# Places of matrices in SBUF: v in products of 448 columns, and the gate's sums by GpSimd and DVE

## The chip, the cores and the metric

The kernel runs on one core of a Trainium2 chip. The metric is the device time of one execution in microseconds (us), the median of several runs. Everything is computed in float32 accuracy. Most products are made from float32r operands that are split in two parts, a high one (the value rounded to float32r) and a low one (the rest), so that one float32 product becomes three float32r products: high by high, high by low, low by high.

## What is computed

```python
x = A_x                                            # 1 x 2048 x 448
g = sigmoid((x * gate_w).sum(-1, keepdims=True))   # one gate for each token
qkv = x @ wqkv                                     # 16 heads of 28
p = softmax(q @ k.T * 28 ** -0.5)
a = (p @ v) @ wo
y = layernorm(x)
b = gelu(y @ w1 + b1) @ w2 + b2                    # 448 -> 1792 -> 448
out = g * a + (1 - g) * b
```

## The kernel before

The tokens are worked in four chunks of 512 (`NC`, `CH`), or in 16 tiles of 128 (`NT`). The kernel has three stages, and within each the order of the instructions on every engine is written out by hand; semaphores alone tie the engines together.

**Stage 1, q, k and v** (to 114 us). For each chunk there are seven tiles of q and k (`qk_tile`, 11 products of 128x512 each, line 220; the first chunk's are at line 322, piece by piece as the data arrives) and four tiles of v (`v_tile`, 11 products each, line 232). In `v_tile` the tokens are the stationary matrix (128x128) and the weights the moving one, 450 columns wide: 448 of v, one with `gate_w`, so that the gate's sum falls out of the same product (line 235 copies it to `zall`), and one of padding. The high and low parts of v's weights lie in two tensors, `wvh` and `wvl`, each with four pieces (of the 448 rows, in 128s) at a distance of 512 columns, that is 2048 bytes in a partition. Beside the products, a list (`at(n, ...)`) puts other work into the slots between the tiles n = 7 to 43: loads and splits of the next chunk's x, the layer norm's statistics by DVE from the token tiles (`stats_fetch`, `ln_stats`, lines 253 and 254), and the first pieces of the MLP's weights. DMAs are issued by SyncE (SP) in program order.

**Stage 2, the MLP** (to 467 us). For each chunk: 14 tiles `mlp1` (11 products of 512 columns, line 613) and then four `mlp2`, one for each 128 tokens. `mlp2` runs over f = 0 to 13 with three products of 448 columns for each f: moving `w2h[f]` with stationary `hh[f]` (line 626), moving `w2l[f]` with stationary `hh[f]` (line 627), moving `w2h[f]` with stationary `hl[f]` (line 631). The places in SBUF follow from the order of allocation: `w2h0, w2l0, w2h1, w2l1, ...`, of 1792 bytes each up to f = 10 and 2048 bytes from f = 11, and `hh[f], hl[f]` of 2048 bytes each from f = 13 down to 0, with a pad of 256 bytes ahead of f = 10 and one of 64 bytes ahead of f = 6 (`SHIFTS`). So `w2h[f]` starts at 0 and `w2l[f]` at 256 within a grid of 512 bytes up to f = 10, and at 0 both from f = 11. `hh[f]` and `hl[f]` start 64 bytes off a grid of 256 bytes for f = 0 to 6, and on it for f = 7 to 13.

Between the MLP's products stand *fillers*: products of q and k whose maxima by row the softmax needs later (line 440; in the MLP stage in bursts of six, `MG`; DVE reduces them, lines 420 and 422). They begin in the first chunk at f = `FS`. Fillers read `khr`, whose load is issued by GpSimd at f = 1 of the first chunk (line 503).

**Stage 3, attention** (to 1097 us, and a tail to 1112 us). Units of (group of heads, query chunk, key tile, head) are worked in rounds of five (`U`), later of seven. A round has three kinds of score products, each 28 or 29 rows deep, several side by side on different row groups of TensorE (line 563): stationary `khi` with moving `qh`, stationary `klo` with moving `qh`, stationary `khi` with moving `ql`; first for the round's first units, then for the last ones. ScalarE takes the exponentials (line 567, two a round). Then follow the products with v (line 830). Fillers stand in this stage too. The projection by `wo` (lines 735 to 737, 12 products of 448 columns for each 128 tokens, moving `woh[g]`, `wol[g]`, `woh[g]`) comes in the last quarter.

All matrices of stage 3, those of `mlp1` and those of q and k start on a grid of 512 bytes. `woh[g]` and `wol[g]` start at the same place within 512 bytes, 0 for g = 0 and 2, 256 for g = 1 and 3.

Of the kernel before, what the change touches and what calls it, by code (L numbers as in the profile page):

```python
# [15 lines left out]
P = 128  # L16
S = 2048
D = 448
# [4 lines left out]
CH = 512  # L23
# [7 lines left out]
MLP_MAX = 482  # L31
MLP_G = MLP_MAX // 260
MG = 6
FS = 4
WARM = 10
W1, W2 = 0.233, 0.205
SHIFTS = {10: 64, 6: 16}
LQ = 12
STEPS = (2, 5, 7, 8, 9, 10)
LSTEPS = (1, 3, 5, 6, 7, 8)  # L40
# [3 lines left out]
def kernel(ctx: ExitStack, tc: tile.TileContext, xt, wqk, wv, wo, xk, w1, b1, w2, b2,  # L44
                          ident_d, sel_d, out):
    nc = tc.nc

    const = ctx.enter_context(tc.tile_pool(name="const", bufs=1))
    dram = ctx.enter_context(tc.tile_pool(name="dram", bufs=1, space=DRAM))
# [6 lines left out]
    zall = const.tile([P, NT], F32, name="zall")  # L56
# [6 lines left out]
    vs = dram.tile([NT, P, NG, P], F32, name="vs")  # L63
    lns = dram.tile([2 * NT, P], F32, name="lns")
    gbs = dram.tile([NT, P, D], F32, name="gbs")
    ones = dram.tile([S // P, P], F32, name="ones")
    rls = dram.tile([NG * NC, 4, CH], F32, name="rls")

# [14 lines left out]
    w1h, w1l, w2h, w2l = {}, {}, {}, {}  # L83
# [73 lines left out]
    with tc.tile_pool(name="qx", bufs=2) as qx, tc.tile_pool(name="qo", bufs=4) as qo, \  # L157
# [8 lines left out]
        def raw():  # L166
            return qx.tile([P, CH], F32, name="raw", bufs=6)
# [14 lines left out]
            nc.scalar.activation(wh[:, m], wt[m], AF.Copy)  # L182
            nc.gpsimd.tensor_sub(wl[:, m], wt[m], wh[:, m].bitcast(F32))

        wvh, wvl = (qw.tile([P, 4, CH], F32R, name=f"wv{x}")[:, :, :450] for x in "hl")
        vt = [qw.tile([P, H, 32], F32, name=f"vt{i}") for i in range(3)]

        xh, xl = {}, {}
        xraw = {}

        def fetch_x(c, t):
            xraw[c, t] = raw()
            nc.sync.dma_start(xraw[c, t], xt[t, :, c * CH:(c + 1) * CH])
# [29 lines left out]
        def v_tile(tt):  # L223
            c, i = divmod(tt, TPC)
            sl = slice(i * P, (i + 1) * P)
            ps = next_ps()
            ops = []
            for t in range(3):
                ops += [(xh[c][:, t, sl], wvh[:, t]), (xh[c][:, t, sl], wvl[:, t]), (xl[c][:, t, sl], wvh[:, t])]
            ops += [(xh[c][:, 3, sl], wvh[:, 3]), (xh[c][:, 3, sl], wvl[:, 3])]  # L230
            for k, (a, b) in enumerate(ops):
                nc.tensor.matmul(ps[:, :450], a, b, start=(k == 0), stop=(k == len(ops) - 1))  # L232
            v = vt[tt % 3]
            nc.scalar.activation(v[:, :, 0:DH], ps[:, :D].rearrange("p (h d) -> p h d", d=DH), AF.Copy)
            nc.vector.tensor_copy(zall[:, tt:tt + 1], ps[:, D:D + 1])
            nc.sync.dma_start(vs[tt], v.rearrange("p (g j) d -> p g (j d)", g=NG))

        one_t = qw.tile([S // P, P], F32, name="one_t")
# [2 lines left out]
        mv = qw.tile([P, NT, 2], F32, name="mv")  # L241
        mr = qw.tile([P, 2, NT], F32, name="mr")

        bxr = {}

        def stats_fetch(i):
            bxr[i] = spare(i % (NF // 2)).rearrange("p a b -> p (a b)")[:, :2 * D].rearrange("p (t d) -> p t d", d=D)
            nc.sync.dma_start(bxr[i], xk[2 * i:2 * i + 2].rearrange("t p d -> p t d"))

        def ln_stats(i):  # L250
            x = bxr.pop(i)
            for n in range(2):
                nc.vector.bn_stats(st[:, 2 * i + n], x[:, n])
                nc.vector.bn_aggr(mv[:, 2 * i + n], st[:, 2 * i + n])

# [34 lines left out]
        wvr = []  # L290
# [2 lines left out]
            nc.sync.dma_start(wvr[t], wv[:, t])  # L293
        for t in range(2):
            fetch_x(1, t)
        for v in vt:
            nc.gpsimd.memset(v[:, :, DH:DH + 1], 1.0)
            nc.gpsimd.memset(v[:, :, DH + 1:32], 0.0)
        banks = [next_ps() for m in range(NM)]
        there, pieces, late, count = [], [], [], [0] * NM  # L300
        for what, i in turns:
            if what == "w":
                if i < 4:
                    split_wqk(i)
# [12 lines left out]
            ops += [("hl", m, t) for m, t in new if t < 3]  # L317
            if i == NM - 1:
                ops += late
            for k, m, t in ops:  # L320
                w, x = wl if k == "lh" else wh, xl[0] if k == "hl" else xh[0]
                nc.tensor.matmul(banks[m], w[:, m, t], x[:, t], start=(count[m] == 0), stop=(count[m] == 10))  # L322
                count[m] += 1
                if m == 0 and count[m] == 11:

                    for n in range(4, NM):
                        split_wqk(n)
                    for n in range(4):
                        nc.scalar.activation(wvh[:, n], wvr[n], AF.Copy)
                        nc.gpsimd.tensor_sub(wvl[:, n], wvr[n], wvh[:, n].bitcast(F32))  # L330
                if count[m] == 11:
                    qk_out(0, m, banks[m])
                    if m in (1, 3):
                        split_x(1, m // 2)
                        fetch_x(1, m // 2 + 2)
# [5 lines left out]
        def at(n, what, *args, to=behind):  # L341
            to[n].append((what, args))
# [6 lines left out]
                at(11 * (c - 1) + 4 + t, split_x, c, t)  # L349
        for i, n in enumerate((11, 12, 13, 14, 19, 20, 21, 22)):  # L350
            at(8 + i if i < 7 else 13, stats_fetch, i, to=ahead)
            at(n, ln_stats, i)
        for t, d in ((ident, ident_d), (b1s, b1), (ones, one_t)):
            at(16, nc.sync.dma_start, t, d, to=ahead)
# [15 lines left out]
        for n in range(NM, 11 * NC):  # L370
            for what, a in ahead[n]:
                what(*a)
            c, m = divmod(n, 11)
# [157 lines left out]
    qs = {}  # L531

    def load_q(n):

        g, c = divmod(n, NC)
        qs[n] = aq.tile([P, CH], F32R, name="qh", bufs=3), aq.tile([P, CH], F32R, name="ql", bufs=3)
        for i in range(2):
            for j in range(4):
                r = (4 * g + j) * DH
                nc.sync.dma_start(qs[n][i][32 * j:32 * j + DH].bitcast(F32), qk[i, r:r + DH, c * CH:(c + 1) * CH])  # L540
# [52 lines left out]
    mw2 = ml.enter_context(tc.tile_pool(name="mw2", bufs=1, reuse_waits="tile"))  # L593
    mh = ml.enter_context(tc.tile_pool(name="mh", bufs=1, reuse_waits="tile"))
    for f in range(NF):
        w2h[f], w2l[f] = (mw2.tile([P, CH if f > 10 else D], F32R, name=f"w2{x}{f}")[:, :D] for x in "hl")
    hh, hl = {}, {}
    more = [mh.tile([P, CH], F32, name=f"more{i}") for i in range(2)]
    for f in reversed(range(NF)):
        if f in SHIFTS:  # L600
            mh.tile([P, SHIFTS[f]], F32, name=f"shift{f}")
        hh[f] = mh.tile([P, CH], F32R, name=f"hh{f}")
        hl[f] = mh.tile([P, CH], F32R, name=f"hl{f}")

# [35 lines left out]
    with texts:  # L640
# [12 lines left out]
        for c in range(NC):  # L653
            for f in range(NF):
                if c == 0:
# [21 lines left out]
            if c == NC - 1:  # L677
                m0.close()
                aq = ctx.enter_context(tc.tile_pool(name="aq", bufs=1, side="right", reuse_waits="tile"))
# [36 lines left out]
    aw = sb("aw", 1)  # L716
    ao = sb("ao", 2)
    woh = aw.tile([P, NG, D], F32R, name="woh")
    wol = aw.tile([P, NG, D], F32R, name="wol")

    b2b = aw.tile([P, D], F32, name="b2b")
    sel = aw.tile([P, P], F32, name="sel")

    outcome = [[aw.tile([P, S], F32R, name=f"o{x}{g}") for x in "hl"] for g in range(NG - 1)]
    acc = {}

# [18 lines left out]
    def finish(g, c, pv):  # L745

        ob = ao.tile([P, CH], F32, name="ob")
        rc = ao.tile([P, CH], F32, name="rc")
        lt = ao.tile([P, CH // 32], F32, name="lt")
        nc.vector.tensor_copy(ob, pv)  # L750
        nc.gpsimd.dma_start(lt, ob[DH:P:32, :])  # L751
        yield True
        nc.vector.reciprocal(lt, lt)
        r = rls[g * NC + c]
        nc.gpsimd.dma_start(r.rearrange("j (a b) -> (j a) b", b=CH // 32), lt)
        for j in range(4):
            nc.gpsimd.dma_start(rc[32 * j:32 * j + 32], r[j].partition_broadcast(32))
        yield True
        if g < NG - 1:
            oh, ol = (x[:, c * CH:(c + 1) * CH] for x in outcome[g])  # L760
        else:
            oh, ol = ao.tile([P, CH], F32R, name="oh", bufs=1), ao.tile([P, CH], F32R, name="ol", bufs=1)
# [72 lines left out]
    with tc.manual_schedule(engines=ENGINES):  # L835
# [3 lines left out]
        at = -1  # L839
# [3 lines left out]
        while u < 4 * steps:  # L843
# [56 lines left out]
            if ended:  # L900
                n = summed // NT - 1
# [62 lines left out]
```

## Time and profile before

| | us |
|---|---|
| runs before (3), median (lowest to highest) | 1114.77 (1114.1 to 1116.31) |
| the profiled execution | 1114.39 |
| span of its profile, first to last instruction | 1112.6 |
| TensorE busy in the span | 1104.5 |
| DVE busy | 741.3 |
| ScalarE busy | 634.7 |
| GpSimd busy | 334.2 |

In the profile PE is TensorE's products and PEld its loads of stationary matrices, which run beside the products. Products are pipelined: the duration that the profile gives for one product, 360 ns and more, holds its latency too. What a product costs in a dense row is the *step*, the distance from its start to the next one's start. In the views below the first two numbers of a row are the start and the length in us, "x" is a count, and a bracket says how long the engine had idled before and what ended that.

### The profile page before, as it was taken

The numbers are of one execution on the slowest core, as the hardware profiler recorded it, in microseconds if no ns is written. First come the engines' busy times: TensorE is split into PE (matmuls) and PEld (weight loads), VectorE is DVE, ScalarE is ACT, GpSimd is POOL, SyncE is SP. The second block draws the span as 40 slices with busy tenths as digits, with TensorE's granted clock in tenths as the row PEclk, the third lists the DMA queues.
The fourth block names the chain that finished last, engine by engine and source line by source line (L and its number), as shares of the span: only waits on it lengthen the run. The fifth ranks groups of instructions, "written<-read, shape, count | busy, mean of one in ns | idle before, by whom it ended". The sixth has DMA issues, their size and how long they took to land.

```text
span 1112.6 us, 19807 instructions
## 1 busy us (share of the span) xinstructions
PE 1104.5 (99%) x8156; PEld 675.4 (61%) x8156; DVE 741.3 (67%) x1030; ACT 634.7 (57%) x660; POOL 334.2 (30%) x354
## 2 busy tenths in 40 slices
PE   9999999999999999999999999999999999999998
PEld 7888777777777767744444444444444444454545
DVE  4553488988988889576676766667667667746103
ACT  5334640331240232287887887877878878847572
POOL 5025664343334331013112221320223024342350
PEclk9999999999999999999999999999999999999999
DMA  7988641011121022162100220012011003002111
GB/s 266 356 275 272 177 123 44 9 47 46 41 56 37 25 63 77 52 159 77 28 20 19 61 75 18 20 28 53 29 56 37 18 20 94 12 26 70 51 36 59
DMA packets 53079, 84.35 MB, mean 76 GB/s; under 512 B 8516, under 2 KB 28500, under 8 KB 52076
## 3 DMA queue, kind: packets, MB, share of 16 engines
q1 hardware_dynamic: 48732, 76.27, 22.0%
q0 software_dynamic: 4256, 6.81, 2.5%
q8 instruction: 64, 1.05, 0.4%
q14 instruction: 27, 0.22, 0.1%
HBM read 56.40 MB, written 26.49 MB: 75 GB/s over the span
## 4 chain that ended last, share of the span: by engine, by line
PE 98%; DVE 1%; ACT 1%; DMA 1%; issue 0%; SPq 0%; ACTq 0%
PE bank L830 22%; PE bank L563 20%; PE bank L440 16%; PE bank L613 13%; PE bank L220 5%; PE bank L631 5%; PE bank L626 4%; PE bank L627 4%; PE bank L232 3%; PE bank L322 1%; PE bank L735 1%; PE bank L736 1%; PE bank L737 1%; DMA raw<-in_xt 1%; ACT khi L567 0%
## 5 line engine op out<-in xcount | busy, mean ns | idle before, releaser
L567 ACT ACTIVATE pt<-bank 128x1536 f32<-128x1536 f32 (+1 forms) x386 | 460.1, 1242 | 121.8 <-PE bank L563 121.8
L420 DVE TENSOR_REDUCE mx<-bank 128x1 f32<-128x512 f32 x618 | 409.6, 687 | 174.3 <-PE bank L440 160.1
L830 PE MATMUL bank<-pt,vg 128*32 128x512 f32 x1942 | 260.4, 602 | 0.0
L422 DVE TENSOR_REDUCE mx<-bank 128x2 f32<-128x1024 f32 x203 | 238.8, 1219 | 29.9 <-PE bank L440 29.6
L440 PE MATMUL bank<-khi,qd 28*128 28x512 f32 x512 | 241.8, 480 | 0.1
L440 PEld LDWEIGHTS bank<-khi,qd 28*128 28x128 f32 x512 | 92.6, 182 | 148.1 <-DVE mx L420 106.0
L563 PE MATMUL bank<-qh,klo 28*128 28x512 f32 x1024 | 174.3, 394 | 0.0
L563 PE MATMUL bank<-qh,khi 29*128 29x512 f32 x768 | 156.5, 481 | 0.8 <-ACT khi L567 0.6
L613 PE MATMUL bank<-y,w1f 128*128 128x512 f32 x616 | 151.9, 398 | 0.0
L613 PEld LDWEIGHTS bank<-y,w1f 128*128 128x128 f32 x616 | 112.7, 188 | 33.1 <-issue 10.9
L563 PE MATMUL bank<-ql,khi 28*128 28x512 f32 x768 | 129.1, 390 | 0.0
L618 POOL TENSOR_TENSOR hl<-h,hh 128x512 fp32r<-128x512 f32 x56 | 72.9, 1301 | 117.6 <-ACT h L617 77.5
L616 ACT ACTIVATE hh<-bank,b1s 128x512 fp32r<-128x512 f32 x56 | 38.6, 689 | 99.0 <-PE bank L613 97.5
L830 PEld LDWEIGHTS bank<-pt,vg 128*32 128x32 f32 x1942 | 44.7, 108 | 78.5 <-issue 78.0
L563 PEld LDWEIGHTS bank<-qh,klo 28*128 28x128 f32 x1024 | 87.5, 185 | 3.5
L637 ACT ACTIVATE h<-bank 128x448 f32<-128x448 f32 x16 | 8.7, 546 | 137.5 <-PE bank L631 103.3
L751 POOL DMA_DIRECT2D lt<-ob x15 | 10.9, 725 | 252.6 <-DVE ob L750 252.6
L631 PE MATMUL bank<-w2h,hl 128*128 128x448 f32 x224 | 84.9, 379 | 0.0
L563 PEld LDWEIGHTS bank<-qh,khi 29*128 29x128 f32 x768 | 60.7, 182 | 39.6 <-ACT pt L567 24.9
L626 PE MATMUL bank<-w2h,hh 128*128 128x448 f32 x224 | 83.2, 371 | 0.0
L627 PE MATMUL bank<-w2l,hh 128*128 128x448 f32 x224 | 81.8, 365 | 0.0
L440 PE MATMUL bank<-khr,qd 28*128 28x512 f32 x512 | 80.4, 467 | 0.9 <-issue 0.7
(135 smaller groups left out, 1296.5 us busy)
## 6 DMA issues: line engine op xcount, KB each, us to landing
qk<-hl SPq DMA_DIRECT2D x28, 512.0 KB
raw<-in_xt SPq DMA_DIRECT2D x16, 256.0 KB
vs<-vt SPq DMA_DIRECT2D x16, 256.0 KB
s<-in_xt SPq DMA_DIRECT2D x16, 256.0 KB
rc<-rls POOLq DMA_DIRECT2D x60, 64.0 KB, 2.2
w1f<-in_xk SPq DMA_DIRECT2D x8, 448.0 KB
gbs<-h SPq DMA_DIRECT2D x16, 224.0 KB
klo<-qk SPq DMA_DIRECT2D x16, 224.0 KB
```

The lines of the kernel that those rows point to most:

```text
L220: nc.tensor.matmul(ps, a, b, start=(i == 0), stop=(i == len(ops) - 1))
L420: nc.vector.reduce_max(self.mx[:, c0:c0 + 1], bank[:, b0], axis=AX)
L422: nc.vector.reduce_max(self.mx[:, c0:c1 + 1:c1 - c0], bank[:, b0:b1 + 1], axis=AX)
L440: nc.tensor.matmul(bank[:, b], self.qds[self.n][r, i * P:(i + 1) * P], khi[self.n // NC][r, k * 512:(k + 1) * 512], start=True, stop=True)
L563: nc.tensor.matmul(bank[:, p], a[r, k * P:(k + 1) * P], b[r], start=(i == 0), stop=(i == 2))
L567: nc.scalar.activation(t, bank[:, at[0]:at[-1] + 1], AF.Exp, scale=SCALE)
L613: nc.tensor.matmul(ps, a, b, start=(i == 0), stop=(i == len(ops) - 1))
L618: nc.gpsimd.tensor_sub(hl[f], h, hh[f].bitcast(F32))
L626: nc.tensor.matmul(a, hh[f][:, sl], w2h[f], start=(f == 0), stop=False)
L627: nc.tensor.matmul(a, hh[f][:, sl], w2l[f], start=False, stop=False)
L631: nc.tensor.matmul(a, hl[f][:, sl], w2h[f], start=False, stop=(f == NF - 1))
L830: nc.tensor.matmul(pv[32 * j:32 * j + 32, :], vg[n // NC][:, k, 32 * j:32 * j + 32], probs.pop(4 * step + j), start=(k == 0), stop=(k == N ...
```

## The change

Six edits, of which the diff below shows the core.

- v's products have 448 columns. The weights' eight pieces lie in one tensor `wvx` without gaps, 1792 bytes each, in the order h0, l0, l1, h1, h2, l2, l3, h3, and start 192 bytes off the grid of 256.
- The gate's sums come from the token tiles that the layer norm's statistics read anyway: GpSimd multiplies each by `gate_w` (`gate_x`, 16 products of 128x448), and DVE sums over the row (16 reductions). The row `gate_w` is brought to all partitions by five more DMAs on SP's queue at the start: four of one column of the weights' tile to DRAM, one that spreads it from there.
- `w2`: all tiles of 1792 bytes, in the order h0, l0, l1, h1, h2, l2, ...; all of `hh` and `hl` 64 bytes off the grid of 256. The pads `SHIFTS` go.
- `woh` and `wol` 256 bytes apart within 512, and the matrices that meet them 64 bytes off the grid.
- `qh` 64 bytes off the grid (`ql`, `khi`, `klo` stay on it).
- `FS` is 5 in place of 4: the fillers begin one f later.

```diff
-FS = 4
+FS = 5
-SHIFTS = {10: 64, 6: 16}
+LINE = 16
...
-        wvh, wvl = (qw.tile([P, 4, CH], F32R, name=f"wv{x}")[:, :, :450] for x in "hl")
+        wvx = qw.tile([P, 8 * D + 4 * LINE], F32R, name="wvx")[:, 3 * LINE:3 * LINE + 8 * D].rearrange("p (i d) -> p i d", d=D)
+        wvh, wvl = ([wvx[:, i] for i in n] for n in ((0, 3, 4, 7), (1, 2, 5, 6)))
+        gwb = qw.tile([P, D], F32, name="gwb")
...
-                nc.tensor.matmul(ps[:, :450], a, b, start=(k == 0), stop=(k == len(ops) - 1))
+                nc.tensor.matmul(ps[:, :D], a, b, start=(k == 0), stop=(k == len(ops) - 1))
-            nc.vector.tensor_copy(zall[:, tt:tt + 1], ps[:, D:D + 1])
...
+        def gate_x(i):
+            for n in range(2):
+                zx[i, n] = qw.tile([P, D], F32, name="zx", bufs=2)
+                nc.gpsimd.tensor_mul(zx[i, n], bxr[i][:, n], gwb)
+
         def ln_stats(i):
             x = bxr.pop(i)
             for n in range(2):
+                nc.vector.reduce_sum(zall[:, 2 * i + n:2 * i + n + 1], zx.pop((i, n)), axis=AX)
                 nc.vector.bn_stats(st[:, 2 * i + n], x[:, n])
...
         for t in range(2):
             fetch_x(1, t)
+        for t in range(4):
+            nc.sync.dma_start(gws[t], wvr[t][:, D:D + 1])
+        nc.sync.dma_start(gwb, gws.rearrange("t p -> (t p)")[:D].partition_broadcast(P))
...
             at(8 + i if i < 7 else 13, stats_fetch, i, to=ahead)
+            at(n - 1, gate_x, i)
             at(n, ln_stats, i)
...
-        qs[n] = aq.tile([P, CH], F32R, name="qh", bufs=3), aq.tile([P, CH], F32R, name="ql", bufs=3)
+        qs[n] = (aq.tile([P, CH + P], F32R, name="qh", bufs=3)[:, LINE:LINE + CH],
+                 aq.tile([P, CH], F32R, name="ql", bufs=3))
...
-        w2h[f], w2l[f] = (mw2.tile([P, CH if f > 10 else D], F32R, name=f"w2{x}{f}")[:, :D] for x in "hl")
+
+        t = {x: mw2.tile([P, D], F32R, name=f"w2{x}{f}") for x in ("lh" if f % 2 else "hl")}
+        w2h[f], w2l[f] = t["h"], t["l"]
...
+    mh.tile([P, LINE], F32, name="shift")
     for f in reversed(range(NF)):
-        if f in SHIFTS:
-            mh.tile([P, SHIFTS[f]], F32, name=f"shift{f}")
...
     woh = aw.tile([P, NG, D], F32R, name="woh")
+    aw.tile([P, 4 * LINE], F32, name="gap")
     wol = aw.tile([P, NG, D], F32R, name="wol")
...
+    aw.tile([P, LINE], F32, name="shift")
     outcome = [[aw.tile([P, S], F32R, name=f"o{x}{g}") for x in "hl"] for g in range(NG - 1)]
```

TensorE's products are the same in number and order, but for the fillers, whose first bursts stand one f later.

More of the change, by code (lines that the diff above doesn't have):

```diff
@@ L65 @@
     gbs = dram.tile([NT, P, D], F32, name="gbs")
+    gws = dram.tile([4, P], F32, name="gws")
     ones = dram.tile([S // P, P], F32, name="ones")
@@ L228, in v_tile @@
             for t in range(3):
-                ops += [(xh[c][:, t, sl], wvh[:, t]), (xh[c][:, t, sl], wvl[:, t]), (xl[c][:, t, sl], wvh[:, t])]
-            ops += [(xh[c][:, 3, sl], wvh[:, 3]), (xh[c][:, 3, sl], wvl[:, 3])]
+                ops += [(xh[c][:, t, sl], wvh[t]), (xh[c][:, t, sl], wvl[t]), (xl[c][:, t, sl], wvh[t])]
+            ops += [(xh[c][:, 3, sl], wvh[3]), (xh[c][:, 3, sl], wvl[3])]
             for k, (a, b) in enumerate(ops):
-                nc.tensor.matmul(ps[:, :450], a, b, start=(k == 0), stop=(k == len(ops) - 1))
+                nc.tensor.matmul(ps[:, :D], a, b, start=(k == 0), stop=(k == len(ops) - 1))
             v = vt[tt % 3]
             nc.scalar.activation(v[:, :, 0:DH], ps[:, :D].rearrange("p (h d) -> p h d", d=DH), AF.Copy)
-            nc.vector.tensor_copy(zall[:, tt:tt + 1], ps[:, D:D + 1])
             nc.sync.dma_start(vs[tt], v.rearrange("p (g j) d -> p g (j d)", g=NG))
@@ L242 @@
         mr = qw.tile([P, 2, NT], F32, name="mr")
-        bxr = {}
+        bxr, zx = {}, {}
         def stats_fetch(i):
@@ L328 @@
                     for n in range(4):
-                        nc.scalar.activation(wvh[:, n], wvr[n], AF.Copy)
-                        nc.gpsimd.tensor_sub(wvl[:, n], wvr[n], wvh[:, n].bitcast(F32))
+                        nc.scalar.activation(wvh[n], wvr[n][:, :D], AF.Copy)
+                        nc.gpsimd.tensor_sub(wvl[n], wvr[n][:, :D], wvh[n].bitcast(F32))
                 if count[m] == 11:
@@ L749, in finish @@
         lt = ao.tile([P, CH // 32], F32, name="lt")
+        if not (g or c):
+            ao.tile([P, 2 * LINE], F32, name="gap", bufs=1)
         nc.vector.tensor_copy(ob, pv)
```

## The prediction

> **What bounds the kernel.** I read the page first (busy shares, the chain by engine), then the chain in order of time, then the timeline of TensorE in the stages that the change touches.
>
> ```profile
> PE 1104.5 (99%) x8156; PEld 675.4 (61%) x8156; DVE 741.3 (67%) x1030; ACT 634.7 (57%) x660; POOL 334.2 (30%) x354
> ...
> PE 98%; DVE 1%; ACT 1%; DMA 1%; issue 0%; SPq 0%; ACTq 0%
> ```
>
> TensorE carries 98% of the chain, so a ns off the step from one product to the next is a ns off the time, and work moved to other engines counts only if it delays TensorE. The chain in order of time gives the steps where nothing interrupts:
>
> ```profile
> 25.02 8.95 PE bank L232 x44
> 33.96 17.49 PE bank L220 x77
> ...
> 113.80 14.77 PE bank L613 x65
> ```
>
> q and k (512 columns): 17.49 / 77 = 227.1 ns a product; the MLP's first half (512) 14.77 / 65 = 227.2; v (450 columns) 8.95 / 44 = 203.4. Now the MLP's second half (448 columns), in its first token tile:
>
> ```profile
> 154.52 0.36 PE L626 MATMUL bank<-w2h,hh 128*128 128x448 f32 x1
> 154.72 0.36 PE L627 MATMUL bank<-w2l,hh 128*128 128x448 f32 x1
> 154.92 0.37 PE L631 MATMUL bank<-w2h,hl 128*128 128x448 f32 x1
> 155.12 0.36 PE L626 MATMUL bank<-w2h,hh 128*128 128x448 f32 x1
> ...
> 158.15 0.36 PE L626 MATMUL bank<-w2h,hh 128*128 128x448 f32 x1
> ...
> 159.62 0.36 PE L626 MATMUL bank<-w2h,hh 128*128 128x448 f32 x1
> ...
> 161.48 0.37 PE L626 MATMUL bank<-w2h,hh 128*128 128x448 f32 x1
> ...
> 463.87 0.37 PE L627 MATMUL bank<-w2l,hh 128*128 128x448 f32 x1
> ...
> 467.11 0.36 PE L631 MATMUL bank<-w2h,hl 128*128 128x448 f32 x1
> ```
>
> From 154.52 to 158.15 stand 18 products (f = 1 to 6): 201.7 ns each. From 159.62 to 161.48 stand nine (f = 8 to 10): 206.7 ns. The shape, the order and the alternation of high and low are the same; what differs is that the stationary `hh` lies 64 bytes off the grid of 256 in the first stretch and on it in the second. So the step depends on place, by 5 ns. The last 16 steps before 467.11, in the stage's last tile, average 202.5 ns.
>
> Two more readings fix the size. From 448 to 512 columns the step grows from about 200 to 227.1, 0.42 ns a column, and 16 columns (64 bytes) are 6.7 ns: exactly what parts 200 from 206.7. I read every step as 200 or one 64-byte piece more. And 448 columns are 1792 bytes, 3.5 times 512. At f = 1 to 6 the moving matrices start at 0, 256, 0 within 512 bytes: twice of three each starts where the one before ended, the third time not. Two steps of 200 and one of 206.7 average 202.2, near the 201.7. Matrices of 512 columns on the grid always continue, and theirs is a flat 227. This rule is a guess: f = 11 to 13 and v, which never continue, should then show 206.7 and v shows 203.4.
>
> **Part by part.**
>
> *v.* 16 tiles of 11 products. If each step falls from 203.4 to 200: 176 x 3.4 = 0.6 us saved. The lower bound is the two columns alone, 176 x 0.83 = 0.15. If the new place is a bad one (206.7), 0.6 lost. I take 0.6, since `wvx` gets both things that the 201.7 stretch has: continuing starts and a distance of 64 bytes (192 in the other sense) from the stationary matrix.
>
> *w2.* Now every start continues (0, 256, 0, then 256, 0, 256), and all of `hh` and `hl` lie 64 bytes off.
>
> ```profile
> L626 PE MATMUL bank<-w2h,hh 128*128 128x448 f32 x224 | 83.2, 371 | 0.0
> L735 PE MATMUL bank<-woh,oh 128*128 128x448 f32 x64 | 24.9, 389 | 0.0
> ...
> 1106.07 0.36 PE L735 MATMUL bank<-woh,oh 128*128 128x448 f32 x1
> ...
> 1108.31 0.37 PE L737 MATMUL bank<-woh,ol 128*128 128x448 f32 x1
> ```
>
> Three lines of 224 are 672 products; from 202.5 to 200 that is 1.7 us. The ends: 0 (places do nothing), 672 x 4.2 = 2.8 lost if all became 206.7. I take 1.7.
>
> *Projection.* Three lines of 64; the last tile's 11 steps take 2.24 us, 203.6 each. To 200: 0.7 us; ends 0 and 192 x 3.1 = 0.6 lost. I take 0.7.
>
> *Attention, qh 64 bytes off.* No product of this stage has an off-grid matrix before, so this is bounded. One round:
>
> ```profile
> 634.90 0.50 PE L563 MATMUL bank<-qh,khr 29*128 29x512 f32 x3
> 635.23 0.41 PE L563 MATMUL bank<-qh,klo 28*128 28x512 f32 x3
> 635.46 0.41 PE L563 MATMUL bank<-ql,khr 28*128 28x512 f32 x3
> 635.69 0.50 PE L563 MATMUL bank<-qh,khr 29*128 29x512 f32 x2
> ...
> 636.03 0.39 PE L563 MATMUL bank<-qh,klo 28*128 28x512 f32 x2
> ...
> 636.26 0.39 PE L563 MATMUL bank<-ql,khr 28*128 28x512 f32 x2
> 636.59 1.06 PE L830 MATMUL bank<-pt,vg 128*32 128x512 f32 x8
> ...
> L567 ACT ACTIVATE pt<-bank 128x1536 f32<-128x1536 f32 (+1 forms) x386 | 460.1, 1242 | 121.8 <-PE bank L563 121.8
> ```
>
> 386 exponentials (some 16 more in smaller groups) at two a round are 200 rounds. A round has six groups of score products, and `qh` streams in four. The steps that aren't lengthened by a fresh load of weights are 230 ns (635.23 to 635.46 to 635.69) against 227 for a lone product, so some groups already pay part of a piece. The best end: four steps a round lose a whole piece, 200 x 4 x 6.7 = 5.3 us. The bad end: `qh` now neither continues from `ql` nor `ql` from it, and all six steps gain a piece, 200 x 6 x 6.7 = 8.0 us. By the nearest row, the 3 ns over 227 on four steps a round, 2.4 us could go; I take half, 1.2 saved, because one place was moved and two kinds of load meet it.
>
> *Fillers one f later.*
>
> ```profile
> 118.94 2.27 POOL L503 DMA_DIRECT2D khr<-qk  x4
> ...
> khr<-qk POOLq DMA_DIRECT2D x4, 224.0 KB, 7.6
> ...
> 128.50 0.50 PE L440 MATMUL bank<-khr,qd 28*128 28x512 f32 x3
> 129.66 0.51 PE L440 MATMUL bank<-khr,qd 28*128 28x512 f32 x3 [0.66 <-issue]
> ...
> 134.85 0.73 PE L440 MATMUL bank<-khr,qd 28*128 28x512 f32 x6
> ```
>
> The first burst splits in two, 1.16 us apart; a later one runs its six in one piece, the second half some 0.33 after the first. The missing quarter of `khr`, issued by 121.21 and 7.6 us under way, explains it. An f takes 11 x 0.227 = 2.5 us, so the burst now starts near 131, past 129.66, and 0.8 us go. Ends: 0 and 0.8. The bursts become 0.7% denser (1.7 of some 247 slots go); DVE at 67% over the span takes that.
>
> *The gate.* GpSimd gets 16 products and DVE 16 reductions for 16 copies of one column.
>
> ```profile
> 16.22 4.98 POOL L330 TENSOR_TENSOR wvl<-w1f,wvh 128x450 fp32r<-128x450 f32 x4
> 77.09 1.65 POOL L134 TENSOR_TENSOR s<-s,lnr 128x512 f32<-128x512 f32 x1 [55.89 <-DMA s<-in_xt]
> ...
> L253 DVE BATCH_NORM_STATS2 st<-w1f 128x6 f32<-128x448 f32 x16 | 9.7, 606 | 0.0
> L235 DVE COPY zall<-bank 128x1 f32<-128x1 f32 x16 | 2.5, 154 | 16.7 <-ACT vt L234 16.7
> ...
> 39.66 0.69 DVE L209 TENSOR_TENSOR hl<-bank,hl 128x512 fp32r<-128x512 f32 x1 [0.33 <-ACT hl L208]
> 68.82 0.69 DVE L209 TENSOR_TENSOR hl<-bank,hl 128x512 fp32r<-128x512 f32 x1 [1.80 <-ACT hl L208]
> ```
>
> GpSimd is idle for 55.9 us from 21 to 77, and 16 x 1.25 (the row at 16.22) = 20 us fit. A reduction of 448 costs about the 0.61 of L253. In the tiles with statistics DVE has 0.33 us to spare of 2.5, and gets 1.2: it falls behind by 0.9 us a tile, some 3.6 us after four, and makes it up in the tiles after (1.8 us idle each). Behind it on DVE are the low parts of q and k (L209), and behind those their DMAs on SP. TensorE has eight banks in turn, some 17 us of products, before it meets an uncopied one. I cost this at nothing; without that cover it would be up to 3.6 us.
>
> *Five DMAs on SP.* They stand behind the loads of x (10.30) and ahead of the first store of q and k (18.24):
>
> ```profile
> 10.30 0.96 SPq L193 DMA_DIRECT2D raw<-in_xt  x2
> 18.24 0.96 SPq L210 DMA_DIRECT2D qk<-hl  x2
> ```
>
> SP waits for v's weights, then for the four small stores to land before it issues the fifth. Queued behind are the stores and the second chunk's last two loads of x; that chunk begins at 33.96. 7 us of SP are free; I cost it at nothing, and a delay of some us more would first be seen as ScalarE waiting for `hl`.
>
> Sum: 0.6 + 1.7 + 0.7 + 1.2 + 0.8 = 5.0 us. The profiled execution took 1114.39, so 1109.4 by its own time; the median of the runs, 1114.77, is 0.4 higher: 1109.8.
>
> **Rivals.**
>
> *Places do nothing; chance 0.2.* The 201.7 and 206.7 would be two states that the row falls into by its timing after a filler, not by place. For it: v misses my rule by half, and f = 11 to 13 don't stand out in the last tile's 202.5. Against it: 5 ns between stretches 1.5 us apart. Then 0.15 (two columns) and 0.8 (fillers) are left: 1113.8, no measurable change. The Trainium skill, "TensorE: Matmul & The Clock Gate", section "Part 2: What happens when you issue a matmul", is on this side: TensorE reads moving and stationary matrices through two independent ports, and loading the next weights takes no read bandwidth from the running product; its gap for 512 columns is 216 ns. The trace disagrees with the figure (227.1), and the stretches of 201.7 and 206.7 speak against the rule.
>
> *qh collides; chance 0.15; slower.* Every one of the six group steps gains a piece: 8.0 lost against 3.8 saved elsewhere, 1119.0. It decides from three steps a round (4.0 us). For it: `ql` stays on the grid, so starts alternate between 64 and 0, and the rule of continuing starts is broken four times a round. Against it: 512 columns show no sensitivity so far, though never tried off the grid.
>
> *Attention gains the whole piece; chance 0.15.* If distance from the stationary matrix is what counts, four steps a round fall by 6.7: 5.3 in place of 1.2, 1105.7.
>
> **Numbers.** The forecast, 0.5, has its own range of 1107.5 to 1112. The range over all leaves out the colliding case: 1104.8 to 1114.8. A measurement of this kernel can tell about 0.2%, 2.2 us. Faster than 1112.5: forecast and full gain, 0.65; same 0.2; slower 0.15.
>
> **What would show it.** Right: v's chain pieces of 44 at 8.80 in place of 8.95; the last 16 steps of the MLP at 3.20 in place of 3.24, without alternation; the projection's last tile at 2.20; the first burst of fillers in one piece; rounds of attention shorter, at the steps that follow a `qh` group. Wrong: 448-column steps that stay near 202.5, longer rounds, TensorE waiting before chunk two (33.96), or DVE named as releaser of score banks in stage 1.

## The result, and the profile after

The changed kernel takes 1119.58 us (median of 6 runs, 1117.55 to 1121.51) against 1114.43 for the kernel before beside it (6 runs, 1113.36 to 1116.31). The ratio is 1.0039, with an interval of 1.0025 to 1.0053. It is slower by 5.2 us; forecast were 5.0 less. The profiled execution took 1121.51, its span is 1119.7.

The page's two lines, busy shares and chain by engine, of the kernel after:

```profile
PE 1108.2 (99%) x8156; PEld 677.6 (61%) x8156; DVE 754.7 (67%) x1030; ACT 633.5 (57%) x660; POOL 352.3 (31%) x370
...
PE 87%; DMA 5%; DVE 5%; issue 2%; ACT 1%; SPq 1%; POOL 0%; DVEq 0%; ACTq 0%
```

TensorE had 98% of the chain and has 87% now. DMA, DVE and "issue" hold the rest, so something that TensorE waits for has come in. The share says where the waits hang, not how long they are: once the chain leaves TensorE, at 91 us, it lies on other engines all the way back, while TensorE is busy for 99% as before. From the starts of the first product of each stage in the two traces (the tail from the last product with v), in us:

| | stage 1 | MLP, first chunk | MLP, chunks 2 to 4 | attention | tail |
|---|---|---|---|---|---|
| before | 113.6 | 83.3 | 263.2 | 637.1 | 15.4 |
| after | 117.8 | 87.2 | 263.2 | 636.6 | 15.0 |

The loss is two pieces of 4 us at the front of the kernel. What the new places were meant to do comes after that, and is small. The profiled execution is the slowest of the six, so its pieces add up to 7.1 us and not to the 5.2 of the medians.

**Stage 1.** Three views of after: the chain in order of time (start, length, what), SP's timeline, and TensorE's timeline in the third chunk.

```profile
15.05 7.18 DMA gws<-w1f
...
25.37 6.93 DMA qk<-hl
...
48.02 8.20 DMA qk<-hl
...
73.88 11.42 DMA qk<-hl
85.40 0.61 ACT hl L211
...
89.79 1.60 DVE xh L207
91.43 12.39 PE bank L223 x46
...
109.08 8.89 PE bank L235 x44
```

```profile
13.32 2.05 SPq L305 DMA_DIRECT2D gws<-w1f  x4
22.31 0.32 SPq L306 DMA_DIRECT2D gwb<-gws  x1
22.67 1.73 SPq L213 DMA_DIRECT2D qk<-hl  x2
```

```profile
89.01 0.39 PE L223 MATMUL bank<-xh,wl 128*128 128x512 f32 x1
91.43 0.50 PE L223 MATMUL bank<-xh,wh 128*128 128x512 f32 x1 [2.03 <-DVE xh L207]
...
93.15 0.63 PE L223 MATMUL bank<-xl,wh 128*128 128x512 f32 x1
93.58 0.63 PE L223 MATMUL bank<-xh,wl 128*128 128x512 f32 x1
```

The last of the four stores of 128 x 1 values is issued at 15.05 and lands 7.18 us later. SP stands still until 22.31, so the first store of q and k goes out at 22.67 (18.24 before). The delay is handed on from one `qk<-hl` store to the next, as ScalarE and DVE wait for `hl` buffers, until it reaches TensorE at 89. (Between the stores the chain also runs through the gate's sums on DVE; e1 below keeps these and has no gap.) There stands a gap of 2.42 us between two starts (2.2 more than a step), and then come products 0.43 us apart in place of 0.23, until 96. By the granted clock (the column behind the five engines) TensorE ran at half speed there, and again behind the stall in the MLP, each time for 3.4 us; two stretches of after:

```profile
92.70:96.10 3.40, 3.40 (x9) 2.64 (x8) 0.69 (x1) 0.70 (x2) 0.81 (x1) 0.50 0.93 255
...
167.80:171.20 3.40, 3.40 (x10) 3.00 (x10) 2.23 (x2) 0.00 (x0) 1.63 (x2) 0.50 0.00 0
```

The Trainium skill, "TensorE: Matmul & The Clock Gate", section "Part 1: The HAM clock gate (the "warmup" mystery)", says that the array falls to half its clock after an idle window of about 3.4 us and comes back after a busy one as long, with 426.7 ns a start at 512 columns in between. The trace agrees with the return and the 427 ns; the idle time ahead of it was 2.0 us in one piece here (the bracket at 91.43), and three of 0.6 to 0.7 there. Nor does such idle time always lead to it: e11 and e2 below have as much without slow products behind it.

The DMA share (column before the last) fits that SP's standstill was not made up: the engines were idle while SP stood, and have little to spare in the 18 us behind. Rows of the stretches 18 to 22 and 22 to 40 us, first before, then after:

```profile
18.00:22.00 4.00, 4.00 (x19) 3.30 (x19) 3.97 (x6) 2.21 (x5) 3.20 (x3) 1.00 0.74 262
22.00:40.00 18.00, 18.00 (x86) 15.78 (x85) 6.54 (x15) 6.00 (x11) 0.00 (x0) 1.00 1.01 356
```

```profile
18.00:22.00 4.00, 4.00 (x19) 3.33 (x18) 4.00 (x6) 2.40 (x5) 3.64 (x3) 1.00 0.03 4
22.00:40.00 18.00, 18.00 (x86) 15.76 (x85) 3.86 (x6) 5.20 (x11) 0.00 (x0) 1.00 0.95 300
```

**The MLP's first chunk.** ScalarE's, DVE's and TensorE's timelines of after:

```profile
120.58 1.28 ACT L630 ACT_TABLE_LOAD   x1 [1.97 <-PE bank L627]
```

```profile
130.32 6.93 DVE L119 TENSOR_TENSOR w2l<-lnr,w2h 128x448 fp32r<-128x448 f32 x1 [3.73 <-ACT w2h L116]
...
163.16 6.87 DVE L434 TENSOR_REDUCE mx<-bank 128x2 f32<-128x1024 f32 x6
```

```profile
135.70 0.73 PE L452 MATMUL bank<-khr,qd 28*128 28x512 f32 x6
...
159.79 0.73 PE L452 MATMUL bank<-khr,qd 28*128 28x512 f32 x6
...
164.43 0.49 PE L452 MATMUL bank<-khr,qd 28*128 28x512 f32 x2 [0.68 <-DVE mx L434]
165.56 0.50 PE L452 MATMUL bank<-khr,qd 28*128 28x512 f32 x2 [0.64 <-DVE mx L434]
166.69 0.50 PE L452 MATMUL bank<-khr,qd 28*128 28x512 f32 x2 [0.63 <-DVE mx L434]
...
168.61 0.57 PE L641 MATMUL bank<-w2l,hh 128*128 128x448 f32 x1
168.98 0.57 PE L645 MATMUL bank<-w2h,hl 128*128 128x448 f32 x1
```

And the same two places, ScalarE's table load and DVE's second low part, before:

```profile
114.45 1.28 ACT L616 ACT_TABLE_LOAD   x1
```

```profile
125.61 1.55 DVE L118 TENSOR_TENSOR w2l<-lnr,w2h 128x448 fp32r<-128x448 f32 x1 [2.59 <-ACT w2h L115]
```

A low part of 448 columns takes DVE 6.93 us, not 1.55. DVE is then without a break until it reduces the fifth burst of fillers, issued at 159.79, from 163.16 on; the sixth burst, wanting the same six banks, stalls TensorE three times. Behind that the steps are 0.37 us in place of 0.20, until 171.2. Why DVE is late, and why it matters only now, was open at this point. The table load stands out: before, it ran right behind the last v tile; after, it waits 1.97 us for TensorE first.

**The steps.** TensorE's timeline of after, the MLP's last tile and the projection:

```profile
465.27 0.37 PE L641 MATMUL bank<-w2l,hh 128*128 128x448 f32 x1
...
467.90 0.36 PE L645 MATMUL bank<-w2h,hl 128*128 128x448 f32 x1
```

```profile
1108.53 0.36 PE L753 MATMUL bank<-woh,ol 128*128 128x448 f32 x1
...
1115.80 0.36 PE L753 MATMUL bank<-woh,ol 128*128 128x448 f32 x1
```

13 steps in 2.63 us are 202.3 ns each; 36 in 7.27 are 201.9; v's 44 in 8.89 are 202.0. Over all steps of the two traces that nothing interrupts, before and after: v 203.3 and 202.2, the MLP's second half 202.6 and 202.2, the projection 203.0 and 202.3. In after these rows settle into 199, 201, 207, again and again; none is a flat 200.

### The profile page after: what moved, and what is told of

It reads as the page before. It is cut to its first block, busy times and chain, and to the rows that moved or that the text cites. A ratio compares the mean times of both kernels' runs of the same rounds, so it can differ in the third digit from the quotient of the medians.

```text
span 1119.7 us, 19837 instructions
## 1 busy us (share of the span) xinstructions
PE 1108.2 (99%) x8156; PEld 677.6 (61%) x8156; DVE 754.7 (67%) x1030; ACT 633.5 (57%) x660; POOL 352.3 (31%) x370
## 4 chain that ended last, share of the span: by engine, by line
PE 87%; DMA 5%; DVE 5%; issue 2%; ACT 1%; SPq 1%; POOL 0%; DVEq 0%; ACTq 0%
PE bank L848 22%; PE bank L576 20%; PE bank L452 15%; PE bank L627 11%; PE bank L645 4%; PE bank L640 4%; PE bank L641 4%; DMA qk<-hl 3%; DVE mx L434 2%; PE bank L223 2%; PE bank L751 1%; PE bank L752 1%; PE bank L753 1%; PE bank L235 1%; DVE w2l L119 1%
## 5 line engine op out<-in xcount | busy, mean ns | idle before, releaser
L645 PE MATMUL bank<-w2h,hl 128*128 128x448 f32 x224 | 85.5, 382 | 0.0
L640 PE MATMUL bank<-w2h,hh 128*128 128x448 f32 x224 | 83.5, 373 | 0.0
L641 PE MATMUL bank<-w2l,hh 128*128 128x448 f32 x224 | 82.3, 367 | 0.0
```

The source lines that it names most:

```text
L640: nc.tensor.matmul(a, hh[f][:, sl], w2h[f], start=(f == 0), stop=False)
L641: nc.tensor.matmul(a, hh[f][:, sl], w2l[f], start=False, stop=False)
L645: nc.tensor.matmul(a, hl[f][:, sl], w2h[f], start=False, stop=(f == NF - 1))
```

## The experiments

Each run's time is compared with the runs of the kernel before on the same chip (1114.29 for the first four, 1114.77 for the next four, 1114.81 for the last three). The three columns on the right are of the one profiled execution of each kernel, and need not add up to the median. In the kernels without the hop through DRAM, stage 1 takes 115.3 to 115.6 us in e4, e7, e8 and e10 and 113.8 to 114.4 in the others: in those four profiles the granted clock is 0.50 for 3.4 us between 8 and 13 us, in the others it isn't. So the chunks say more than the spans.

| kernel | time | against before | 95% interval of the ratio | stage 1 | first chunk | attention |
|---|---|---|---|---|---|---|
| e1_direct | 1117.40 | +3.1 | 1.0015 to 1.0038 | 114.3 | 87.2 | 636.4 |
| e2_nogate | 1117.78 | +3.5 | 1.0020 to 1.0044 | 113.8 | 85.6 | 636.4 |
| e3_fs4 | 1114.67 | +0.4 | 0.9993 to 1.0011 | 117.9 | 83.5 | 636.3 |
| e4_places | 1113.88 | -0.4 | 0.9989 to 1.0006 | 115.6 | 83.6 | 636.3 |
| e5_fs5 | 1114.05 | -0.7 | 0.9983 to 1.0001 | 114.4 | 82.3 | 637.2 |
| e6_direct_fs4 | 1113.97 | -0.8 | 0.9983 to 1.0001 | 113.9 | 83.4 | 636.5 |
| e7_direct_fs6 | 1114.29 | -0.5 | 0.9986 to 1.0004 | 115.3 | 82.3 | 636.4 |
| e8_direct_late | 1114.68 | -0.1 | 0.9993 to 1.0011 | 115.5 | 82.9 | 636.4 |
| e9_direct_early | 1112.71 | -2.1 | 0.9974 to 0.9991 | 113.8 | 82.3 | 636.5 |
| e10_direct_khr | 1120.36 | +5.6 | 1.0033 to 1.0060 | 115.4 | 85.5 | 636.5 |
| e11_after_early | 1114.38 | -0.4 | 0.9985 to 1.0003 | 116.4 | 82.4 | 636.5 |

**e1_direct: the gate's weights by one DMA.** The row comes as an input of its own; stores and DRAM buffer go.

```diff
-        for t in range(4):
-            nc.sync.dma_start(gws[t], wvr[t][:, D:D + 1])
-        nc.sync.dma_start(gwb, gws.rearrange("t p -> (t p)")[:D].partition_broadcast(P))
+        nc.sync.dma_start(gwb, gw.partition_broadcast(P))
```

> The changed kernel, but gate_w is one more input and is spread to all partitions by one DMA from DRAM, in the place of the four one-column stores and the fifth DMA behind them. Theory 1 (the small stores take 7 us to land, SP and the DMA engines stand idle behind them, and the delay reaches the last chunk's x): the MLP begins near 113.3 us of the span as before the change (113.6) and not at 117.8; total 4 us or more below the changed kernel, near 1115. Theory 2 (DVE's 16 reductions put the low parts of x late): it still begins near 117 to 118, and the total stays near 1119.

SP's timeline of this kernel:

```profile
12.44 0.33 SPq L303 DMA_DIRECT2D gwb<-in_gw  x1
19.10 0.96 SPq L212 DMA_DIRECT2D qk<-hl  x2
```

The first store of q and k is back at 19.10 and TensorE's gap in the third chunk is gone: stage 1 takes 114.3 for 117.8. The first chunk stays at 87.2. So the two losses are separate, and the hop's is shown. By the medians it is 2.0 us (5.2 less 3.1), half of the 4 that were expected from the profile of after: there the slow products behind the gap are in it too.

**e2_nogate: no gate sums at all.** The gate's DMAs, GpSimd's products and DVE's reductions are left out (`zall` is zero).

```diff
-            at(n - 1, gate_x, i)
...
-                nc.vector.reduce_sum(zall[:, 2 * i + n:2 * i + n + 1], zx.pop((i, n)), axis=AX)
```

> The changed kernel without the gate's sums: no gate row, no products on GpSimd, no reductions; the sums are set to zero, so that the gate is one half for every token. Theory 1 and theory 2 both expect the MLP to begin at 113.0 to 113.4. What this takes less than the kernel with the direct DMA is the price of GpSimd's and DVE's part: 0 by theory 1, 3 to 4 us by theory 2. If the first MLP chunk still takes 87.2 us (83.3 before), its loss does not come from the gate.

1117.78 against e1's 1117.40: the sums by GpSimd and DVE cost nothing that can be measured. The long low part (6.99 us) is here too, so it isn't the gate's doing. So are the three waits of TensorE behind it, the last of them in this row:

```profile
162.63 0.49 PE L447 MATMUL bank<-khr,qd 28*128 28x512 f32 x2 [0.63 <-DVE mx L429]
```

But the steps behind them stay at 0.20 us, and the first chunk takes 85.6 us where e1 has 87.2. So of the loss in this chunk 3.3 us go with the waits (85.6 against 82.3 in e9), and 1.6 with the slow clock, which comes or doesn't.

**e3_fs4: the changed kernel with the old start of the fillers.**

```diff
-FS = 5
+FS = 4
```

> The changed kernel with FS = 4, so that the fillers begin at the f where they began before the change. If the later fillers make the first MLP chunk long (87.2 us in place of 83.3), it falls back to 83 to 84 us and the total by 3.5 us, to 1116; if it is GpSimd holding DVE off (one low part of w2 took 6.9 us), the chunk stays at 86 to 88 us, or gets longer by the 0.8 us wait for khr, and the total stays at 1119 to 1120.

1114.67, where 1116 was expected; the first chunk came as expected. Stage 1 still has its 117.9, in a profiled execution of 1117.26. DVE's low part takes 5.68 us even so, and no stall follows. Starting one f later is what makes the late DVE costly.

**e4_places: the kernel before with the new places of w2, hh, hl, wo and qh alone.**

```diff
-SHIFTS = {10: 64, 6: 16}
+LINE = 16
...
-        w2h[f], w2l[f] = (mw2.tile([P, CH if f > 10 else D], F32R, name=f"w2{x}{f}")[:, :D] for x in "hl")
+        t = {x: mw2.tile([P, D], F32R, name=f"w2{x}{f}") for x in ("lh" if f % 2 else "hl")}
+        w2h[f], w2l[f] = t["h"], t["l"]
```

> The kernel before with the places alone: w2, hh, hl, wo, its outcomes and qh as in the change; v with 450 columns in its old places, the gate from it, FS = 4. By the steps of the changed kernel's trace (202.2 for 202.6 in the MLP, 202.3 for 203.0 in the projection, attention 0.5 us shorter): 0.5 to 1.3 us less than the kernel before, 1113.5. By the prediction's rule of continuing starts: 3.6 less. If the places also cost waits (the table load of ScalarE that came 1.3 us late at the MLP's start), up to 4 us more.

The places are worth 0.4 us, inside the interval of no change. Their steps are those of after (second half of the MLP 202.2, projection 202.3). But this kernel has the late table load as well, and a low part of 5.75 us, in 83.6 us for the first chunk.

**e5_fs5: the kernel before with FS = 5 alone.** Counting the filler's slots by its own sums in the code gave a candidate: with a start at 4 the fifth burst comes in the last tile of `mlp1`, with a start at 5 at f = 4 of `mlp2`'s first tile, behind the eight low parts that are issued in between.

```diff
-FS = 4
+FS = 5
```

> Kernel before with one number changed: the maxima (fillers) may start at f = 5 instead of 4; places, v's 450 columns and the gate as before. Worked out from the filler's own sums in the code: bursts of six come in f = 5, 7, 9, 11, 13 of mlp1 and then at f = 7 and 12 of mlp2's first tile with a start at 4; with a start at 5 in f = 6, 8, 10, 12 of mlp1, and the fifth at f = 4 of mlp2's first tile, right behind the eight low parts that DVE and GpSimd still owe, the sixth at f = 9. Theory A (it is this place of the fifth burst): first chunk of the MLP 86 to 88 us as in the changed kernel, in the old places too, mlp2's first tile over 13 us against 10.3, time 1117 to 1119. Theory B (the new places of w2, hh and hl bring it): first chunk at most 83.5, time 1113 to 1114.5.

Theory A, the place of the burst alone, falls: 82.3 us, the shortest first chunk so far. The burst is where the count says, and DVE is in time for it (second row, 0.52 us idle before the low part):

```profile
126.40 1.54 DVE L118 TENSOR_TENSOR w2l<-lnr,w2h 128x448 fp32r<-128x448 f32 x1 [2.59 <-ACT w2h L115]
...
155.34 1.12 DVE L118 TENSOR_TENSOR w2l<-s,w2h 128x448 fp32r<-128x448 f32 x1 [0.52 <-ACT w2h L115]
156.38 3.48 DVE L422 TENSOR_REDUCE mx<-bank 128x2 f32<-128x1024 f32 x3
```

The time is theory B's, but e3 and e4 have the new places and lose nothing in the first chunk. So it takes both, the late DVE of the new places and the late start: theory D, tested by e9.

**e6_direct_fs4: e1 with FS = 4.**

```diff
-FS = 5
+FS = 4
```

> Changed kernel with the gate's weights fetched as an input of their own (one DMA instead of four stores and a spread) and the fillers starting at f = 4. If the two losses add up (the hop through DRAM some 2 to 3.5 us, the late start some 4 to 5): stage 1 about 114.3, first chunk 83.3 to 83.6, attention 636.3, time 1112 to 1113, 0.1 to 0.2% under the kernel before. Rival (the gate's multiplies and sums cost time once the rest is mended, and the places bring nothing): 1114 to 1115.

Chunk and attention came as expected, the time 1 us above, at the rival's edge: no gain that could be told from none. Here DVE's low part takes 5.71 us, and DVE catches up.

**e7_direct_fs6: e1 with FS = 6.**

```diff
-FS = 5
+FS = 6
```

> As the kernel with its gate weights as an input of their own, but the fillers start at f = 6, one later than in the changed kernel. By the filler's sums the bursts come in f = 7, 9, 11, 13 of mlp1 and then at f = 7 and 12 of mlp2's first tile: none right behind the eight low parts. Theory A (place of the fifth burst): first chunk 82.3 to 83.6, no gaps over 1 us in mlp2's first tile, no wait for khr in f = 5, time 1111.8 to 1113.2. Theory C (the later the start, the worse, since the bursts then stand 2% closer or DVE starts with a longer backlog): first chunk 87 or more, time 1117.4 to 1120.

The first chunk is 82.3, with a low part of 6.97 us. DVE's rows of the last low part and of the burst behind it:

```profile
157.55 1.58 DVE L118 TENSOR_TENSOR w2l<-s,w2h 128x448 fp32r<-128x448 f32 x1
159.59 3.49 DVE L431 TENSOR_REDUCE mx<-bank 128x2 f32<-128x1024 f32 x3 [0.46 <-PE bank L449]
```

The burst at f = 7 finds DVE idle. Not "the later the worse": 5 is bad, 4 and 6 are not. Its time, 1114.29, is 1 us over what was expected. In the profiled execution (1115.42) stage 1 took 115.3, with the slow clock at its start, and chunks 2 to 4 about 1 us more than in e1; why the median is over stays open.

**e8_direct_late: FS = 5 kept, but the first tile of mlp2 takes fillers from f = 7.**

```diff
-            rows = not last and (c * TPC + i < NT - 2 or f < 10) and (c + i > 0 or f > 3)
+            rows = not last and (c * TPC + i < NT - 2 or f < 10) and (c + i > 0 or f > 6)
...
-                        filler.spread(nc.sync, MLP_MAX, 11 * W1 * (0.65 * (NF - FS) + 3 * NF) + W2 * (3 * NF * (NT - 1) - 24))
+                        filler.spread(nc.sync, MLP_MAX, 11 * W1 * (0.65 * (NF - FS) + 3 * NF) + W2 * (3 * NF * (NT - 1) - 33))
```

> As the kernel with its gate weights as an input of their own, fillers from f = 5 as in the changed kernel, but mlp2's first tile takes fillers only from f = 7 on instead of f = 4 (the count of slots is lowered by the nine that go). The fifth burst then comes three f (1.9 us) later. Theory A: DVE is through with its low parts by about 3 us after the old place, so most of the wait of 3.3 us and the slow products behind it go: first chunk 83.5 to 85, time 1114 to 1116. Theory C (the backlog of DVE is there anyway, the stall only moves): first chunk about 87, time 1117 to 1118.

82.9, a little better than expected, with one wait of 0.62 us left. Moving one burst by three f takes away 4.3 us of the first chunk.

**e9_direct_early: one small Gelu ahead.** In the compiled program ScalarE's queue at the first `mlp1` tile reads, before and after:

```text
before: wait DMA; wait DMA, DVE; load table; Gelu hh0 (waits TensorE)
after:  wait DVE; wait DMA, TensorE; load table; Gelu hh0 (waits ScalarE)
```

In the new places `hh0` lies on memory that ScalarE itself wrote, as the wait for its own semaphore indicates. In both kernels one wait stays with the Gelu and the others stand ahead of it; the one that stays is now ScalarE's own, and TensorE's has moved ahead of the table load. A Gelu of one column behind the last v tile loads the table early and is meant to change nothing else:

```diff
             for what, a in behind[n]:
                 what(*a)
+        nc.scalar.activation(gate[:, 0:1], eps_t, AF.Gelu_apprx_tanh)
```

> Kernel with the gate weights as an input of their own, fillers from f = 5, new places, and one small Gelu on ScalarE behind the last v tile (into a cell of gate that is overwritten later), so that the table for Gelu is loaded before the first product of mlp1 is awaited. Theory D (two things together: in the new places the first Gelu's wait for TensorE stands ahead of the table load, which puts ScalarE 1.28 us and then DVE some 6 us behind, and with a start at 5 the fifth burst comes right behind the low parts, where DVE can't make it up): the 0.58 us gap at mlp1's third tile goes, the second w2 low part takes 1.5 us instead of 6.9, first chunk 82.3 to 82.8 against 87.2, time 1112.5 to 1113.5. Rival (the table load is a side effect, the hold-off comes from the order of GpSimd's work): only the gap of 0.5 goes, first chunk 86.5 or more, time about 1117.

ScalarE, DVE and TensorE of this kernel:

```profile
114.56 1.28 ACT L389 ACT_TABLE_LOAD   x1
```

```profile
125.72 1.58 DVE L118 TENSOR_TENSOR w2l<-lnr,w2h 128x448 fp32r<-128x448 f32 x1 [2.54 <-ACT w2h L115]
...
155.73 3.49 DVE L432 TENSOR_REDUCE mx<-bank 128x2 f32<-128x1024 f32 x3
```

```profile
159.08 0.73 PE L450 MATMUL bank<-khr,qd 28*128 28x512 f32 x6
```

All as theory D says: low part 1.58, first chunk 82.3, sixth burst in one piece. At 1112.71 this is 5.2 us faster than e1, each against its own runs of before, and 0.17% faster than the kernel before (interval 0.09 to 0.26%). It beats both kernels.

**e10_direct_khr: table load left late, khr's four DMAs issued by SP.** GpSimd's timeline of the kernel after shows it at work without a break while DVE's low part hangs:

```profile
124.45 2.27 POOL L515 DMA_DIRECT2D khr<-qk  x4
...
129.23 1.31 POOL L109 TENSOR_TENSOR w1f<-more,w1f 128x512 fp32r<-128x512 f32 x1
...
135.49 1.27 POOL L632 TENSOR_TENSOR hl<-h,hh 128x512 fp32r<-128x512 f32 x1
```

```diff
-                        load_khr(0, queue=nc.gpsimd)
+                        load_khr(0)
```

> Kernel with the gate weights as an input of their own, fillers from f = 5, new places, table load left late, but the four DMAs of khr issued by SP instead of GpSimd, which takes 2.27 us off GpSimd at mlp1's third tile. If DVE's 6.9 us low part is DVE being held off while GpSimd runs five two-input operations back to back: GpSimd has idle time between them again, the low part takes under 3 us, first chunk 83.0 to 84.5 (the 0.46 us of the late table load stays, SP's fetches of w2 come up to 1.7 us later), time 1113.4 to 1115. If the low part is long for another reason (the data it reads come late): 6.9 us again, first chunk about 87, time about 1117.

DVE's, GpSimd's, ScalarE's and TensorE's timelines of this kernel:

```profile
127.94 1.35 DVE L118 TENSOR_TENSOR w2l<-lnr,w2h 128x448 fp32r<-128x448 f32 x1 [4.06 <-ACT w2h L115]
```

```profile
127.53 1.29 POOL L629 TENSOR_TENSOR hl<-h,hh 128x512 fp32r<-128x512 f32 x1
128.78 1.67 POOL L108 TENSOR_TENSOR w1f<-s,w1f 128x512 fp32r<-128x512 f32 x1
```

```profile
131.61 0.63 ACT L105 ACTIVATE w1f<-lnr 128x512 fp32r<-128x512 f32 x1 [3.69 <-DMA lnr<-in_w]
```

```profile
133.44 2.60 PE L624 MATMUL bank<-y,w1f 128*128 128x512 f32 x10 [2.32 <-ACT h L628]
```

The low part takes 1.35 us with the table load as late as ever, and the stall in `mlp2`'s first tile is gone: DVE was held off by GpSimd. In after (6.93 us) and in e3 (5.68) it ends 0.5 us after GpSimd first stops, in e3 for no more than 0.23 us. What differs in e10 is not that GpSimd has a gap: it works without one from 125.03 to 130.45. DVE gets in between two of its instructions, and the second takes 1.67 us in place of 1.29. In before, e5, e9, e10 and e11, where DVE gets in so, this low part starts 0.2 to 0.4 us after the start of a GpSimd instruction; in the eight kernels where it is held, 1.0 to 1.1 us after. That this moment decides was not tested.

The time missed all the same, 1120.36. On SP's queue `khr` stands ahead of two fetches of weights, ScalarE waits 3.69 us for one, and TensorE for ScalarE; hence 85.5. The other 5.6 us come after the last product: the tail takes 20.8 us against 15.2 in e1, though the four output stores are issued as early and their bytes have moved as soon. What the program waits for there isn't in the trace, and stays open.

**e11_after_early: the changed kernel with that one Gelu.**

```diff
+        nc.scalar.activation(gate[:, 0:1], eps_t, AF.Gelu_apprx_tanh)
```

> The changed kernel itself with the one small Gelu behind the last v tile, the gate weights still through DRAM. By theory D what is left of its loss is the hop alone (stage 1 117.3 to 118, 2.2 us by the medians, 3.5 by the profiles): first chunk 82.3 to 82.8, time 1114.8 to 1116.4. By its rival 1119.

1114.38, a little under what was expected, with the first chunk at 82.4. One line gives back the 5.2 us. What is left against e9, 1.7 us, is the hop through DRAM, whose gap in the third chunk is still there:

```profile
91.67 0.50 PE L223 MATMUL bank<-xh,wh 128*128 128x512 f32 x1 [2.18 <-DVE xh L207]
```

The products behind it stay 0.23 us apart here, and stage 1 takes 116.4 us where after has 117.8.

## Why the prediction was wrong

The sign was lost on two steps that the sum put at nothing, the five DMAs on SP and the bursts that DVE "takes", together with a cost that it doesn't have, the late table load. Most of its gains were too large as well.

*v, w2, projection (0.6, 1.7, 0.7 forecast).* The failed step is the rule, called a guess there, that a step is a flat 200 once every matrix starts where the former ended. All starts continue now, and one step in three still costs the 6.7 more. Measured: v 176 x 1.1 = 0.2 us (of the 1.1 ns some 0.8 are the two columns fewer, by the prediction's 0.42 ns a column), w2 672 x 0.38 = 0.3, the projection 192 x 0.7 = 0.1. The stretches at 206.7 did go; but the mean was 202.5 already, which the forecast had quoted and then aimed 2.5 below.

*qh (1.2).* Right in kind and half in size: 0.5 to 0.9 us less in the kernels with the new place (636.3 to 636.6) than in the two without (637.1, 637.2). The step from `qh` on `klo` to `ql` fell from 234 to 232 ns (median), where it was looked for. That the total lies near the 1119.0 of the colliding rival is chance: attention got shorter.

*Fillers one f later (0.8).* The wait for `khr` went, and the first burst stands in one piece (135.70); alone it is worth 1.0 us of the first chunk (e5) and 0.7 of the time, which the interval doesn't tell from none. The failed step is the next sentence, that DVE "at 67% over the span takes" the denser bursts. The density was not the matter. One f moves the fifth burst across the end of `mlp1` and behind eight low parts, where DVE has 0.5 us to spare (e5) and can't make up the 5.4 that it lost. A share over the span says nothing of that place.

*What was not on the list.* No step asked what the new places do to the waits. Moving `hh0` onto a tile that ScalarE wrote changed which wait stands ahead of the table load; ScalarE came 1.28 us late, the moment at which DVE's low part meets GpSimd's row of work moved, and DVE lost 5.4 us in one instruction (6.93 against 1.55). e9 and e11 show that this doesn't happen without the late load, e4 that the load is late by the places alone. The Trainium skill, "SBUF — State Buffer", section "Who interferes with whom", has the last link: a DVE instruction with two SBUF inputs contends with a GpSimd instruction that reads SBUF, and the order of issue decides which of them blocks. The trace agrees that DVE blocks, but the wait is longer than one GpSimd instruction: DVE's lasted over five of them. With FS = 4 or 6 the first chunk takes 82.3 to 83.5 us in spite of this backlog (e3, e6, e7), with FS = 5 and no backlog 82.3 (e5, e9); both together cost some 5 us of the time (e1 against e9 5.2, after against e3 4.8, each to its own runs of before).

*The gate.* Costed at nothing, and it is (e1 against e2).

*Five DMAs on SP.* Costed at nothing, since "7 us of SP are free". This failed: four stores of half a kilobyte each took 7.2 us to land, SP's free time ended 4.4 us late, and the DMA engines, at a share of 0.03 meanwhile, have a share of 0.95 in the 18 us that follow, so little is made up. Cost 1.2 to 2.0 us (e3 against e6 1.2, e11 against e9 1.7, after against e1 2.0, each to its own runs of before). The sign named for it, ScalarE waiting for `hl`, is the one that came.

The forecast's own range had no case in which a queue's wait and an engine's backlog act at once; its one slower rival was about places.

## What to carry to other kernels

When a tile moves to other memory, look at the waits that change owner as well as at the addresses: a wait that moves ahead of a table load can cost more than the places bring. Load an activation table by a dummy instruction where the engine idles, not at first use. Before a burst of work is moved by one slot, list what the engine that must answer it has queued there; its mean share is no guide, and a store that must land before its queue goes on is to be priced by landing, not by issue.

## What the runs showed that was not expected

- Four stores of 128 x 1 values from SBUF to DRAM, issued over 2.05 us, landed 7.2 us after the last, with the DMA engines nearly idle for the last 4.
- GpSimd can hold DVE off over five GpSimd instructions in a row: 6.93 us for one operation of 1.55. In e9 and e10 GpSimd had no gap either, and DVE got in behind one instruction (1.58 and 1.35).
- 2.0 us of idle TensorE, or three waits of 0.6 to 0.7 us within 3 us, were followed by 3.4 us at a granted clock of 0.50 in after, and the like (2.2 us in e11, the three waits in e2) by none. One such stretch is worth 1.6 us (87.2 against 85.6).
- Steps of 448 columns repeat 199, 201, 207 ns in v, the MLP's second half and the projection alike; their means lie at 202.1 to 202.3 in the kernels with the new places.
